# Gates on GpSimd with powers and Newton steps, five y pairs in the key sweep, and w2 steps 0, 6 and 13 as seven products

## The chip, the cores and the metric

The kernel runs on one core of one Trainium2 chip. Its time is device microseconds of that core, and the figure compared is the median of several runs. The profile is one execution taken by the hardware profiler; its span runs from the first instruction to the last.

Names of the engines, as the profile has them: PE is TensorE (matmuls), PEld its weight loads, DVE is VectorE, ACT is ScalarE, POOL is GpSimd, SP is SyncE, which issues most of the DMAs. All matmuls of the large products are float32 split into a high and a low part (fp32r tiles), so that one float32 product costs several matmuls.

## What is computed

```python
x = A_x                                     # 1 x 2048 x 576
g = sigmoid((x * gate_w).sum(-1))           # one gate per token
a = linear_attention(x, wqkv, wo)           # 32 heads of 18
y = layernorm(x)
b = gelu(y @ w1 + b1) @ w2 + b2             # 576 -> 4608 -> 576
out = g * a + (1 - g) * b
```

Here `layernorm` divides by `sqrt(var + 1e-5)`, `gelu` is the tanh form, and the attention uses `phi(t) = where(t > 0, t + 1, exp(t)) + 1e-6` on queries and keys.

## The kernel before

**Stages.** The 2048 tokens are 16 tiles of 128, in two halves of 8 tiles ("sup" 0 and 1). The kernel runs a key sweep over the 16 tiles (projections of keys and queries, `phi`, and the sums of keys by tokens), then a short stage that turns the sums into one weight matrix, then an attention stage over the 16 tiles (`attend`, lines 844 to 861), and then the large part, the two-layer product. Each turn of the key sweep over tile n has three thirds, numbered 3n, 3n+1 and 3n+2; the table `jobs` (line 560) holds closures that are run at the end of a third. So work that is not part of the sweep is put into it by number: the gates of a group of tiles (`gates_in`, `gates_act`, `gates_out`, `share_moments`), and the preparation of normalized inputs, called y, for the first half. In the last three turns of the sweep the queries are left for later, so these turns are shorter.

**The y pairs.** One y pair is two token tiles, one of each 512-token block. `load_pair` (SP) brings the raw rows and their mean and reciprocal deviation; `normal_pair` does four 128x768 DVE operations, `sum_pair` four 128x384 DVE operations; `split_pair` copies high parts on ACT and subtracts them for the low parts on DVE, `split_tails` does the last rows on DVE, and `store_pair` writes the result to HBM. `Y_JOBS` (line 77) gives the thirds. The four pairs of the first half are made in the sweep; the four pairs of the second half are made by `make_y` (line 1287) inside the large part.

**The gates.** `gates_in` (line 362) takes the maximum for the sigmoid and the variance; `gates_act` (line 369) does `Exp` and `Sqrt` on ACT, each with its own table, and an `Exp` on a spare element to bring the first table back; `gates_out` (line 376) does reciprocals and one Newton step for the reciprocal root on DVE. Four groups of two tiles run in the sweep and one group of eight in the attention stage (`MOMENTS`, line 34).

**The large part.** For each half of the tokens, 18 chunks of the 4608 columns are done; a chunk of one half is a step k, 0 to 35. A step has two streams of matmuls. The up stream (`product`) is y times w1, seven products (a Strassen-like scheme of 2x2 blocks) of seven 128x512 matmuls. The down stream is gelu(...) times w2. A step in the set `SEVEN` (line 84) does it as seven products too: 14 units of six 128x288 matmuls (`one_of_seven`). Any other step does it plainly: 8 units of twelve (`plain_unit`). Before the change steps 0, 6, 13 and 35 are plain. The seven products need sums of the blocks of h (`make_sum`) and of w2 (`sum_w2`), and more high and low parts (tiles `h` and `region`). A step in both `SEVEN` and `FIVES` adds some products together in PSUM first, with copies on ACT, and then needs 8 evictions by DVE (`accs<-ps,accs`); a step in `SEVEN` alone needs 12; a plain one 5, and step 0 plain 8.

**The order of the large part** is written by a planner in the kernel (`plan`, line 1420): every operation is an `Op` with an engine, a cost from a table, what it needs and what it gives; a due time is reckoned backward from the matmul streams; the operation to be placed next is chosen by start and due time. `TUNED` (line 89) holds its weights, `ON_DVE` and `DVE_SUMS` say which sums go to DVE and which to POOL (`sum_on`, line 1024). What it gives is a fixed order of instructions for each engine. Two PSUM pairs (banks 6 and 7, banks 4 and 5) take the down units in turn, so a unit waits until the eviction of the unit two before it is done.

Of the kernel before, what the change touches and what calls it, by code (L numbers as in the profile page):

```python
# [17 lines left out]
P = 128  # L18
# [15 lines left out]
MOMENTS = ((0, 2), (2, 4), (4, 6), (6, 8), (8, 16))  # L34
# [1582 lines left out]
```

## Time and profile before

| what | value |
|---|---|
| median of 3 runs | 1095.69 us (1095.6 to 1096.69) |
| span of the profiled execution | 1094.1 us; the page gives no other time for it |
| PE busy | 1087.8 us, 99% of the span, 6694 instructions |
| PEld busy | 996.8 us, 91% |
| DVE busy | 917.2 us, 84% |
| ACT busy | 687.5 us, 63% |
| POOL busy | 235.6 us, 22% |
| mean granted clock of PE | 0.999 of full speed |

A busy time is the union of the instructions' spans. Matmuls are pipelined and each span holds the passage through the array, so that one 128x288 matmul reads 296 ns while the next starts 131 to 132 ns after it; PE at 99% says that matmuls follow each other all the time, not that none of them starts late. The median of the runs lies 1.6 us above the profiled span.

### The profile page before, as it was taken

The numbers are of one execution on the slowest core, as the hardware profiler recorded it, in microseconds if no ns is written. First come the engines' busy times: TensorE is split into PE (matmuls) and PEld (weight loads), VectorE is DVE, ScalarE is ACT, GpSimd is POOL, SyncE is SP. The second block draws the span as 40 slices with busy tenths as digits, with TensorE's granted clock in tenths as the row PEclk, the third lists the DMA queues.
The fourth block names the chain that finished last, engine by engine and source line by source line (L and its number), as shares of the span: only waits on it lengthen the run. The fifth ranks groups of instructions, "written<-read, shape, count | busy, mean of one in ns | idle before, by whom it ended". The sixth has DMA issues, their size and how long they took to land.

```text
span 1094.1 us, 18599 instructions
## 1 busy us (share of the span) xinstructions
PE 1087.8 (99%) x6694; PEld 996.8 (91%) x6694; DVE 917.2 (84%) x1553; ACT 687.5 (63%) x1230; POOL 235.6 (22%) x232
## 2 busy tenths in 40 slices
PE   9999999999999999999999999999999999999998
PEld 9999999999898889988889999989899999999898
DVE  4568784895799999899999997988887888878888
ACT  6677765454667887777877876455545555455552
POOL 2111112531123232332111202121122211221110
PEclk9999999999999999999999999999999999999999
DMA  6466772745745565764556559574444435444432
GB/s 186 128 88 190 171 218 102 286 173 188 252 152 195 184 206 192 235 215 161 199 174 222 195 192 395 174 253 119 138 145 118 130 119 150 132 119 119 135 100 87
DMA packets 109006, 189.72 MB, mean 173 GB/s; under 512 B 8940, under 2 KB 68604, under 8 KB 104818
## 3 DMA queue, kind: packets, MB, share of 16 engines
q1 hardware_dynamic: 108002, 187.78, 53.3%
q8 instruction: 53, 0.87, 0.3%
q10 hardware_dynamic: 720, 0.74, 0.2%
q14 instruction: 39, 0.32, 0.1%
q0 software_dynamic: 192, 0.01, 0.1%
HBM read 121.70 MB, written 66.80 MB: 172 GB/s over the span
## 4 chain that ended last, share of the span: by engine, by line
PE 93%; DVE 3%; DMA 1%; ACT 1%; issue 0%; SPq 0%; ACTq 0%; DVEq 0%
PE ps L120 93%; DVE accs L120 1%; DMA s<-in_wm 0%; DVE h L120 0%; DMA fresh<-in_ue 0%; DMA ystage<-late_acc 0%; ACT u L120 0%; DMA s<-in_we 0%; DVE wp L120 0%; DVE region L120 0%; SPq L120 0%; DVE den L120 0%; DVE fresh L120 0%; DVE ystage L120 0%; DVE u L120 0%
## 5 line engine op out<-in xcount | busy, mean ns | idle before, releaser
L120 PEld LDWEIGHTS ps<-region,h 128*128 128x128 f32 x3072 | 437.8, 188 | 30.1 <-ACT ps L120 4.3
L120 PE MATMUL ps<-region,h 128*128 128x288 f32 x3072 | 457.1, 296 | 1.0 <-DVE region L120 0.4
L120 DVE TENSOR_TENSOR accs<-ps,accs 128x576 f32<-128x576 f32 x330 | 246.1, 753 | 60.9 <-PE ps L120 54.1
L120 PE MATMUL ps<-y,wa 128*128 128x512 f32 x1008 | 257.6, 393 | 0.0
L120 PEld LDWEIGHTS ps<-y,wa 128*128 128x128 f32 x1008 | 180.9, 188 | 30.3 <-ACT ps L120 0.2
L120 POOL TENSOR_TENSOR fresh<-fresh 128x288 f32<-128x288 f32 (+1 forms) x128 | 116.4, 913 | 410.5 <-DMA fresh<-in_w 129.6
L120 PE MATMUL ps<-y,wb 128*128 128x512 f32 x756 | 199.3, 394 | 0.1
L120 DVE TENSOR_TENSOR h<-u,h 128x512 fp32r<-128x512 f32 x240 | 165.9, 704 | 8.7 <-ACT u L120 8.7
L120 PEld LDWEIGHTS ps<-y,wb 128*128 128x128 f32 x756 | 133.9, 188 | 20.9 <-ACT u L120 0.5
L120 ACT ACTIVATE region<-fresh 128x576 fp32r<-128x576 f32 (+1 forms) x132 | 81.3, 625 | 73.5 <-PE ps L120 72.9
L120 PE MATMUL ps<-y 128*128 128x288 f32 (+1 forms) x896 | 125.8, 297 | 0.3 <-DVE y L120 0.2
L120 PEld LDWEIGHTS ps<-y 128*128 128x128 f32 x896 | 122.6, 189 | 1.8 <-DVE y L120 0.4
L120 ACT ACTIVATE ps<-ps 128x576 f32<-128x576 f32 (+1 forms) x127 | 78.7, 621 | 45.0 <-PE ps L120 21.5
L120 POOL TENSOR_TENSOR u<-u 128x512 f32<-128x512 f32 x44 | 57.0, 1296 | 193.5 <-DVE h L120 54.9
L120 DVE TENSOR_TENSOR region<-fresh,region 128x576 fp32r<-128x576 f32 (+1 forms) x132 | 93.8, 723 | 1.1 <-ACT region L120 1.1
L120 ACT ACTIVATE u<-ps 128x512 f32<-128x512 f32 x73 | 43.0, 589 | 68.4 <-PE ps L120 68.2
L120 ACT ACTIVATE h<-u 128x512 fp32r<-128x512 f32 x128 | 73.5, 622 | 10.0 <-DVE u L120 5.5
L120 ACT ACTIVATE h<-u,b1s 128x512 fp32r<-128x512 f32 x73 | 52.6, 722 | 42.6 <-DVE u L120 42.4
L120 PE MATMUL ps<-wp,qt 128*128 128x288 f32 x448 | 63.0, 297 | 0.0
L120 DVE TENSOR_TENSOR u<-ps,u 128x512 f32<-128x512 f32 x74 | 50.4, 683 | 13.5 <-PE ps L120 12.7
L120 PEld LDWEIGHTS ps<-wp,qt 128*128 128x128 f32 x448 | 59.8, 188 | 0.0
L120 DVE TENSOR_TENSOR u<-u 128x512 f32<-128x512 f32 x84 | 58.1, 691 | 1.7 <-POOL u L120 1.1
(137 smaller groups left out, 1052.1 us busy)
## 6 DMA issues: line engine op xcount, KB each, us to landing
w1d<-wa SPq DMA_DIRECT2D x17, 1280.0 KB
wa<-w1d SPq DMA_DIRECT2D x68, 320.0 KB
fresh<-in_w SPq DMA_DIRECT2D x70, 288.0 KB
y<-yd SPq DMA_DIRECT2D x14, 1280.0 KB
w1d<-wb SPq DMA_DIRECT2D x17, 960.0 KB
wb<-w1d SPq DMA_DIRECT2D x51, 320.0 KB
yd<-ystage SPq DMA_DIRECT2D x28, 320.0 KB
fresh<-in_um SPq DMA_DIRECT2D x64, 128.0 KB
```

What stands on the lines that cost most here:

```text
L120: self.last = self.tc.keep_in_program_order(op(*args, **kwargs))
```

## The change

It does these things:

1. The gates move from DVE to POOL: 3 small operations in `gates_in` and 11 in `gates_out`. The reciprocal and the reciprocal root are powers (`OP.pow` with exponents -1 and -0.5 from a small tile), each followed by a Newton step. ACT keeps one `Exp` per group; its `Sqrt` and the spare `Exp` go, and with them 9 of 11 table loads.
2. Gates come in groups of two tiles for ten tiles, and one group of six in the attention stage; before there are four groups of two and one of eight.
3. Five y pairs are made in the key sweep, one every six thirds; the fifth is the first pair of the second half, so `make_y` makes three. The high part of a piece (ACT) is put a third ahead of its low part (DVE).
4. Steps 0, 6 and 13 join `SEVEN`. `FIVES` gains 6, 13 and 17 and loses 16.
5. The planner gets other constants (`HEAR_NS`, a cost for a run of matmuls of one stream, `EACH`), other weights, and a choice of POOL or DVE for every single sum.

```diff
-MOMENTS = ((0, 2), (2, 4), (4, 6), (6, 8), (8, 16))
+MOMENTS = ((0, 2), (2, 4), (4, 6), (6, 8), (8, 10), (10, 16))
-Y_JOBS = ((13, (16, 16, 17, 17), (18, 18, 19, 19), (18, 19, 20, 21)), ...
...
+Y_JOBS = ((9, 14, (16, 16, 17, 17), (18, 18, 19, 19), (18, 19, 19, 20), (19, 20, 20, 21)), ...
...
-SEVEN = set([1, 2, 3, 4, 5, 7, 8, 9, 10, 11, 12, 14, 15, ...
+SEVEN = set([0, 1, 2, 3, 4, 5, 6, 7, 8, 9, 10, 11, 12, 13, 14, 15, ...
...
+HEAR_NS = {"PE": 155, "ACT": 65, "DVE": 65, "POOL": 110, "DMA": 300}
...
-FIVES = set([1, 2, 3, 4, 5, 7, 8, 9, 10, 11, 12, 14, 15, 16])
+FIVES = set([1, 2, 3, 4, 5, 6, 7, 8, 9, 10, 11, 12, 13, 14, 15, 17])
...
     def gates_in(b):
...
-        dve.tensor_scalar(ve, sumsq[:, own], 1 / D, EPS_LN, op0=OP.mult, op1=OP.add)
+        pool.tensor_scalar(ve, sumsq[:, own], 1 / D, EPS_LN, op0=OP.mult, op1=OP.add)
...
     def gates_act(b):
...
         act.activation(g[:, own], g[:, own], AF.Exp, scale=-1.0)
-        act.activation(rstd, ve, AF.Sqrt)
-        if MOMENTS[b][1] < NT:
-            act.activation(tiny, ones[:, 0:1], AF.Exp)
...
     def gates_out(b):
...
+        pool.tensor_scalar(omg[:, own], g[:, own], 1.0, None, op0=OP.add)
+        pool.tensor_tensor(out=g[:, own], in0=omg[:, own], in1=powers[:, 0:1].to_broadcast([P, n]), op=OP.pow)
...
+        pool.tensor_tensor(out=rstd, in0=ve, in1=powers[:, 1:2].to_broadcast([P, n]), op=OP.pow)
+        pool.tensor_tensor(out=vr, in0=rstd, in1=rstd, op=OP.mult)
+        pool.tensor_tensor(out=vr, in0=vr, in1=ve, op=OP.mult)
+        pool.tensor_scalar(vr, vr, -0.5, 1.5, op0=OP.mult, op1=OP.add)
+        pool.tensor_tensor(out=rstd, in0=rstd, in1=vr, op=OP.mult)
...
-    for b, n in enumerate((9, 13, 22, 28)):
-        at(n, gates_in, b)
-        at(n + 1, gates_act, b)
-        at(n + 2, gates_out, b)
-        at(n + 2, share_moments, b)
...
+    for pair, (gated, loaded, normal, added, high, low) in enumerate(Y_JOBS):
+        sup, j = divmod(pair, TPB)
+        at(gated, gates_in, pair)
+        for step in (gates_act, gates_out, share_moments):
+            at(gated + 1, step, pair)
...
-    HEAR = {PE: 155, ACT: 33, DVE: 33, POOL: 78, DMA: 30}
+    HEAR = HEAR_NS
...
-        own = ((what, k, m) in ON_DVE) != ((m, k < NCHUNK) in DVE_SUMS)
+        own = (what, k, m) in ON_DVE
...
-        for j in range(TPB):
+        for j in range(len(Y_JOBS) - TPB, TPB):
             dma(lambda j=j: load_pair(1, j), raw_free["rows"], [("yraw", j)], 5600, 7, each=700)
...
```

How instructions move, at three places.

PE at the start of the large part (`ps<-y,wa` and `ps<-y,wb` are the up stream, `ps<-region,h` the down stream, first of step 0). Before:

```order
L120 MATMUL ps<-y,wa 128x512 x28
L120 MATMUL ps<-y,wb 128x512 x21
L120 MATMUL ps<-y,wa 128x512 x28
L120 MATMUL ps<-region,h 128x288 x12
L120 MATMUL ps<-y,wb 128x512 x7
L120 MATMUL ps<-region,h 128x288 x24
L120 MATMUL ps<-y,wb 128x512 x7
L120 MATMUL ps<-region,h 128x288 x12
```

and with the change:

```order
L120 MATMUL ps<-y,wa 128x512 x28
L120 MATMUL ps<-y,wb 128x512 x21
L120 MATMUL ps<-y,wa 128x512 x25
L120 MATMUL ps<-region,h 128x288 x6
L120 MATMUL ps<-y,wa 128x512 x3
L120 MATMUL ps<-y,wb 128x512 x4
L120 MATMUL ps<-region,h 128x288 x6
L120 MATMUL ps<-y,wb 128x512 x3
```

Units of twelve became units of six, 84 matmuls in the step for 96. In all of the program 3036 of them stand where 3072 stood; no other matmul group changed its count.

POOL in the sweep, from the addition of one tile's keys to the next (`pks<-pks,k`), around the first gates. Before:

```order
L120 MEMSET kvs 126x1152
L120 TENSOR_TENSOR pks<-pks,k 128x576
L120 DMA moments_116<-mr_110 128x4x1
L120 TENSOR_TENSOR pks<-pks,k 128x576 x2
L120 DMA moments_117<-mr_111 128x4x1
```

and with the change:

```order
L120 TENSOR_TENSOR pks<-pks,k 128x576
L120 COPY mr_113<-nmean 128x2
...
L120 TENSOR_SCALAR omg<-g 128x2
L120 TENSOR_TENSOR g<-omg,powers 128x2
L120 TENSOR_TENSOR mt<-omg,g 128x2
L120 TENSOR_SCALAR mt<-mt 128x2
L120 TENSOR_TENSOR g<-g,mt 128x2
L120 TENSOR_SCALAR omg<-g 128x2
L120 TENSOR_TENSOR mr_113<-mt,powers 128x2
...
L120 DMA moments_120<-mr_113 128x4x1
```

Between the addition and the DMA of the moments stand 14 small operations that stood on DVE before.

DVE at the end of the sweep, the last turn but one and the keys of the last (`ys` and `y<-accs` are low parts and tails of a y pair, `xs`, `ks` and `k` belong to the sweep). Before:

```order
L120 SCALAR_TENSOR_TENSOR ks<-k,ks 128x576
L120 TENSOR_TENSOR xs<-xn,xs 128x512
L120 TENSOR_TENSOR xs<-xn,xs 128x64
L120 TENSOR_TENSOR ys_561<-accs,ys_561 128x2x256
L120 SCALAR_TENSOR_TENSOR ys_561<-ys_561,low_rows,accs 128x2x128
L120 TENSOR_TENSOR ys_562<-accs,ys_562 128x2x256
L120 SCALAR_TENSOR_TENSOR ys_562<-ys_562,low_rows,accs 128x2x128
L120 TENSOR_TENSOR y<-accs,y 128x256
L120 SCALAR_TENSOR_TENSOR y<-y,low_rows,accs 128x128
L120 SCALAR_TENSOR_TENSOR k<-ps,e 128x288 x2
```

and with the change:

```order
L120 SCALAR_TENSOR_TENSOR ks<-k,ks 128x576
L120 TENSOR_TENSOR xs<-xn,xs 128x512
L120 TENSOR_TENSOR xs<-xn,xs 128x64
L120 TENSOR_TENSOR accs<-accs 128x384 x4
L120 TENSOR_TENSOR ys_565<-accs,ys_565 128x2x256
L120 SCALAR_TENSOR_TENSOR ys_565<-ys_565,low_rows,accs 128x2x128
L120 TENSOR_TENSOR ys_566<-accs,ys_566 128x2x256
L120 SCALAR_TENSOR_TENSOR ys_566<-ys_566,low_rows,accs 128x2x128
L120 TENSOR_TENSOR ys_567<-accs,ys_567 128x2x256
L120 SCALAR_TENSOR_TENSOR ys_567<-ys_567,low_rows,accs 128x2x128
L120 SCALAR_TENSOR_TENSOR k<-ps,e 128x288 x2
```

The four sums of the pair now stand in this turn, ahead of three low parts with their tails; the four 128x768 operations stand in the turn before.

Counts on DVE, from the order, between the first low part of h and the first operation that finishes an output tile of the first half (`accs<-accs,omg`): evictions `accs<-ps,accs` 133 before and 140 now, low parts of h 121 and 128, of w2 49 and 54 (128x576) and 15 and 18 (128x288), sums of h (`u<-u`) 36 and 40, of w2 (`fresh` 128x288) 32 and 40, of w1 (`fresh` 128x384) 28 and 32; of a y pair `accs<-accs` 128x768 16 and 12, 128x384 16 and 12, `ystage` 128x256 28 and 21, `ystage` 128x128 28 and 21. On POOL, up to its last sum of w1: sums of w1 36 and 32, of w2 20 and 27, of h 20 and 28. In the rest of the program DVE has 0 and 33 sums of w2 and 48 and 34 of h; POOL has 72 and 35 of w2 and 24 and 38 of h.

## Rows read from the trace of the kernel before

**Rows 1.** The page, part 4: shares of the span on the chain that ended last

```profile
PE 93%; DVE 3%; DMA 1%; ACT 1%; issue 0%; SPq 0%; ACTq 0%; DVEq 0%
```

**Rows 2.** Busy time by stretch; in brackets the count of instructions

```profile
core 0: us, PE busy (x) PEld busy (x) DVE busy (x) ACT busy (x) POOL busy (x), PEclk, DMA share, GB/s
25.00:175.00 150.00, 150.00 (x991) 143.45 (x991) 106.41 (x231) 106.42 (x238) 22.82 (x18) 1.00 0.63 164
...
275.00:300.00 25.00, 25.00 (x132) 21.70 (x131) 19.50 (x32) 16.91 (x28) 3.26 (x4) 1.00 0.76 255
300.00:650.00 350.00, 349.21 (x2063) 313.37 (x2062) 336.62 (x564) 268.44 (x444) 86.29 (x80) 1.00 0.56 190
650.00:700.00 50.00, 50.00 (x301) 45.15 (x300) 41.72 (x64) 32.73 (x56) 11.65 (x12) 1.00 0.84 318
...
575.00:600.00 25.00, 25.00 (x157) 23.04 (x156) 25.00 (x43) 19.28 (x31) 3.02 (x3) 1.00 0.60 212
```

**Rows 3.** Timeline of PE, 305 to 312 us: start, length, operation, count

```profile
306.91 1.74 PE L120 MATMUL ps<-region,h 128*128 128x288 f32 x12
308.48 1.76 PE L120 MATMUL ps<-y,wa 128*128 128x512 f32 x7
```

**Rows 4.** Timeline, 540 to 573 us; in square brackets idle time before, and its releaser

```profile
563.55 0.56 DVE L120 TENSOR_TENSOR fresh<-fresh 128x384 f32<-128x384 f32 x1 [1.28 <-DMA fresh<-in_ue]
...
564.05 0.42 PE L120 MATMUL ps<-region,h 128*128 128x288 f32 x2
...
564.83 0.80 PE L120 MATMUL ps<-region,h 128*128 128x288 f32 x4 [0.35 <-DVE region L120]
```

**Rows 5.** Weight loads, 275 to 700 us: busy, mean ns, idle before, what ended it

```profile
L120 PEld LDWEIGHTS ps<-region,h 128*128 128x128 f32 x1553 | 220.5, 188 | 16.3 <-ACT ps L120 4.0 <-DVE region L120 0.6 <-ACT ystage L120 0.4
```

**Rows 6.** Groups of DVE, 300 to 650 us, by form

```profile
L120 DVE TENSOR_TENSOR accs<-ps,accs 128x576 f32<-128x576 f32 x111 | 81.7, 750 | 5.4 <-PE ps L120 5.0
L120 DVE TENSOR_TENSOR h<-u,h 128x512 fp32r<-128x512 f32 x99 | 68.1, 700 | 0.0
L120 DVE TENSOR_TENSOR region<-fresh,region 128x576 fp32r<-128x576 f32 x42 | 34.8, 834 | 0.5 <-ACT region L120 0.5
L120 DVE TENSOR_TENSOR wa<-fresh,wa 128x512 fp32r<-128x512 f32 x30 | 22.2, 740 | 0.9 <-ACT wa L120 0.9
...
L120 DVE TENSOR_TENSOR wb<-fresh,wb 128x768 fp32r<-128x768 f32 x16 | 16.4, 1022 | 2.4 <-ACT wb L120 2.2
...
L120 DVE TENSOR_TENSOR fresh<-fresh 128x288 f32<-128x288 f32 x31 | 14.9, 481 | 0.0
L120 DVE TENSOR_TENSOR accs<-accs 128x768 f32<-128x768 f32 x16 | 14.9, 947 | 0.0
...
L120 DVE TENSOR_TENSOR ystage<-accs,ystage 128x256 fp32r<-128x256 f32 x27 | 11.2, 416 | 0.0
L120 DVE SCALAR_TENSOR_TENSOR ystage<-ystage,low_rows,accs 128x128 fp32r<-128x128 f32 x27 | 10.7, 396 | 2.6 <-ACT ystage L120 2.6
...
L120 DVE TENSOR_TENSOR accs<-accs 128x384 f32<-128x384 f32 x16 | 9.6, 601 | 0.0
```

**Rows 7.** Timeline, 540 to 573 us, a POOL operation and DVE beside it

```profile
546.43 1.03 POOL L120 TENSOR_TENSOR fresh<-fresh 128x384 f32<-128x384 f32 x1 [0.75 <-DVE region L120]
...
546.89 1.12 DVE L120 TENSOR_TENSOR h<-u,h 128x512 fp32r<-128x512 f32 x1
```

**Rows 8.** Timeline of POOL, the key sweep, one tile to the next

```profile
77.91 1.42 POOL L120 TENSOR_TENSOR pks<-pks,k 128x576 f32<-128x576 f32 x1 [5.61 <-DVE k L120]
89.10 1.43 POOL L120 TENSOR_TENSOR pks<-pks,k 128x576 f32<-128x576 f32 x1 [9.77 <-DVE k L120]
```

**Rows 9.** Timeline, 156 to 181 us, the end of the key sweep

```profile
173.22 0.81 DVE L120 TENSOR_TENSOR xs<-xn,xs 128x512 fp32r<-128x512 f32 x2
...
176.88 0.86 PE L120 MATMUL ps<-xs,ks 128*128 128x512 f32 x3
```

**Rows 10.** Tile mr: the matmul that turns the last group's moments

```profile
L120 PE MATMUL ps<-accs,mr x1: 273/273/273, 231.1 to 231.1; 128*16 128x128 f32 x1
```

More of the change, by code (lines that the diff above doesn't have):

```diff
@@ L161, in tile_gated_mix @@
     dve.memset(ones, 1.0)
+    powers = keep.tile([P, 2], F32, name="powers")
+    pool.memset(powers[:, 0:1], -1.0)
+    pool.memset(powers[:, 1:2], -0.5)
     tiny = keep.tile([P, 1], F32, name="tiny")
@@ L428, in tile_gated_mix, with split_pair, high_pair @@
     ys = {}
-    def split_pair(sup, j, part, stage, width=2):
+    def split_pair(*args):
+        high_pair(*args)
+        low_pair(*args[:3])
+    def high_pair(sup, j, part, stage, width=2):
         m0, m1 = width * part, min(width * part + width, 7)
@@ L435, in split_pair, with low_pair @@
         act.activation(to[:, :, 0:3], src, AF.Copy)
+    def low_pair(sup, j, part):
+        _, _, src, to = ys[sup, j, part]
         dve.tensor_sub(to[:, :, 3:5], src[:, :, 0:2], raw(to[:, :, 0:2]))
@@ L557, in tile_gated_mix @@
     y_stages.append(y_place.rearrange("p (m s n) -> p m s n", m=2, s=5))
-    jobs = {n: [] for n in range(3 * NT)}
+    jobs = {n: [] for n in range(3 * NT + 3)}
     def at(n, f, *args):
@@ L1418, in tile_gated_mix, with plan @@
     assert len(in_order) == len(ops)
-    def plan(lag, late, slop, slack, guard, ahead, second=None):
-        second = second or (lag, late, slop, slack, guard, ahead)
+    def plan(lag, late, slop, slack, guard, ahead, second, hold, wait):
         slot, due = {o: n for n, o in enumerate(ups)}, {}
@@ L1444, in plan, with streams @@
         port_at, moved, landed = {e: 0 for e in port_until}, 0.0, []
-        next_up, next_down, shift = 0, 0, 0.0
+        next_up, next_down, shift, run = 0, 0, 0.0, ["", 0]
+        def streams(o):
+            n = round(o.ns / (231.7 if o.by[0] == "up" else 132.3))
+            each, more = EACH[o.by[0]]
+            at_ = run[1] if run[0] == o.by[0] else 0
+            return n, n * each + sum(more[at_:at_ + n])
         def offer(o):
@@ L1493, in choose @@
                     if ta is not None and tb is not None:
-                        if tb <= ta + 100:
+                        if tb <= ta + 100 and not (run[0] == "up" and run[1] < hold and behind < wait and ta <= free[PE]):
                             ta = None
@@ L1523, in plan @@
             s, _, o = min(picks, key=lambda x: x[:2])
-            e, t = o.engine, s + o.tail
+            e, t, ns = o.engine, s + o.tail, o.ns
             if e == PE:
+                n, ns = streams(o)
+                t += ns - o.ns
+                run[:] = o.by[0], n + (run[1] if run[0] == o.by[0] else 0)
                 shift = s - nominal[o]
@@ L1530, in plan @@
                         late, slop, slack, guard = second[1:5]
+                        hold, wait = second[6:8]
                 else:
```

55 lines of the change are left out of this document (28 added, 27 removed).

## The prediction

> **What bounds the kernel now.** I read the chain of waits first: it lies on PE for 93% of the span [rows 1], so time is won by fewer matmuls, by matmuls that start earlier, or not at all. Then the table by stretch [rows 2]: PE is busy without a gap in the key sweep (25 to 175 us) and in the large part, at a granted clock of 1.00. A busy PE hides small delays, since each span holds the passage through the array; so the third view is the timeline of PE, where the spacing is to be read from the starts: twelve 128x288 matmuls take from 306.91 to 308.48, 131 ns each [rows 3].
>
> The fourth view is what makes PE late. At 564.05 two matmuls start, the next ones should come at 564.31 and come at 564.83, 0.52 us late; DVE had waited 1.28 us for a DMA just before [rows 4]. The idle time before the weight loads of the down stream between 275 and 700 us sums what waits cost there: 4.0 for ACT's copies in PSUM, 0.6 for DVE's low parts of w2, 0.4 for others, 5.0 us [rows 5]. That is an upper bound for what PE loses, as loads run ahead of their matmuls. The reader is to see the second resource too: DVE is busy 336.6 of 350 us between 300 and 650 [rows 2]. Of its 13.4 us of idle time there, 5.0 are waits for PE before evictions (DVE is ahead), and the others on the rows are 0.4, 0.5, 0.9, 2.4 and 2.6, with the DMA wait of 1.28 some 8.1 us of waits that it did not choose [rows 4, 6]. In the second half it has room.
>
> A measurement of this kernel can tell about 0.2%, 2.2 us, from no change.
>
> **The change part by part.**
>
> *36 matmuls fewer.* Steps 0, 6 and 13 need 84 down matmuls in place of 96. At 131 ns [rows 3] that is 36 x 0.131 = 4.7 us, and all of it lies on PE, the bound: -4.7. The Trainium skill (TensorE: Matmul & The Clock Gate, section Back-to-back issue gap) gives an isolated gap of N/2.4 + 2.5 ns, 122.5 ns for 288 columns, so an estimate by that page would be 4.4 us for this term; the trace has 131, which I use.
>
> *DVE in the first half of the large part.* The order gives what stands between the first low part of h and the first finished tile. Added: 7 evictions at 0.750, 7 low parts of h at 0.700, 5 of w2 at 0.834 and 3 narrow ones, priced as the sums of the same width at 0.481, 4 sums of h at 0.700 (same columns as the low part), 8 sums of w2 at 0.481, 4 sums of w1 at 0.56 [rows 4, 6]: 5.3 + 4.9 + 4.2 + 1.4 + 2.8 + 3.8 + 2.2 = 24.6 us. Gone with one y pair: 4 x 0.947, 4 x 0.601, 7 x 0.416 and 7 x 0.396 = 3.8 + 2.4 + 2.9 + 2.8 = 11.9 us [rows 6]. Net +12.7 us of DVE, slightly high since operations overlap by a little, while PE's time for the same stretch falls by 4.7.
>
> Does it fit? If everything fell between 300 and 650, DVE would want 336.6 + 12.7 + 8.1 of unchosen waits = 357.4 us where PE wants 350 - 4.7 = 345.3: 12.1 us too much. Against that stand 5.5 us of idle DVE in 275 to 300 and 8.3 in 650 to 700 [rows 2], into which work can move (a good third of the added work belongs to step 0, at the front), and the 8.1 themselves: 21.9 us in all. So the cover is there, but more than half of it is needed. That PE can run beside a full DVE is shown by 575 to 600: DVE 25.00 of 25, PE 25.00 [rows 2]. Bounds of this term beyond the 4.7: all late starts gone, -5.0; nothing moved or saved, 357.4 against the 350 of before, +7.4 and the 4.7 given back, that is +12.1. I take -0.5: the new table reckons a DMA 300 ns later than before instead of 30, which strikes the one 0.52 us late start that a late DMA made [rows 4]; the other late starts I keep, as a fuller DVE makes new ones as readily as it loses old ones.
>
> *The second half of the large part.* DVE gets 33 w2 sums there, and POOL 14 more of h; PE has no late starts of note in it and DVE is not the bound. Cost 0; the room hides it, and with the room gone it would cost what the first half's rows say, 0.481 a sum.
>
> *The fifth y pair in the sweep.* DVE had 106.4 of 150 us there [rows 2]. One pair is 4 x 0.947 + 4 x 0.601 = 6.2, and low parts and tails of about the length of the seven each above, 5.7 at most: +11.9, less the 44 gate operations. In the long turns, 43.6 us of idle DVE hide it. The end is tight: the last three turns have no queries. There DVE gets, in the last turn but one, four sums (2.4) for one tail moved away (0.8), and in the turn before four long operations (3.8) for four sums and about one part (2.4 + 1.2, less one part of the pair now before it): some 2 to 3 us later in all. The last tile's low parts end at 173.22 + 0.81 = 174.03, the matmuls that need them start at 176.88 [rows 9], a cover of 2.85. I take +0.3; bounds 0 and 2.7.
>
> *High part a third ahead of the low.* DVE no longer waits for the ACT copy directly ahead of it; nobody on PE waits for either. Cost 0.
>
> *Gates on POOL.* The trace has no power. A POOL operation takes 1.03 us for 384 columns and 1.42 for 576 [rows 7, 8], 2 ns a column and 0.25 us at no columns. Fourteen operations of two columns: 3.5 us at that price; bound from above, two powers at the cost of a full 576-column operation: 6 us. Behind them wait the next addition of keys, one tile (11.2 us, from 77.91 to 89.10) later [rows 8], and `load_pair` on SP, four thirds of a tile later, 14.9 us. What SP holds behind `load_pair` is input for a tile that is three tiles off. So 0, with 8 us to spare; if a power took over 5 us, SP would be late. In the attention stage the moments' matmul stands at 231.1 [rows 10], two to three tiles behind the gates, and POOL waits there for DVE. Again 0. What ACT gains by fewer table loads is off the chain: 0.
>
> **Sum.** Against the profiled execution, 1094.1: -4.7 - 0.5 + 0.3 = -4.9, so a span of 1089.2. The median of the runs stands 1.6 over that span, so **1090.8 us**.
>
> **The rivals.**
>
> *PE's late starts vanish.* The finer choice of engine for each sum would feed PE in time. For: 5.0 us of waits are few and short [rows 5]. Against: DVE gets fuller. Time: 1095.7 - 4.7 - 5.0 = 1086.0. Chance 0.18.
>
> *DVE takes back the gain.* Part of the 12.1 us finds no place. With 5 to 8 us of it left over, the time is 1090.8 + 0.5 + (2.5 to 6.5): 1093.5 to 1097.8, no difference to be told. For: idle time of DVE at 3.8%, more than half unchosen [rows 2, 6]. Chance 0.15.
>
> *POOL blocks DVE, and DVE becomes the bound.* This one ends on the other side. A subtraction of h that takes 0.700 on average took 1.12 us when it started at 546.89, within a POOL sum that ran from 546.43 to 547.46 [rows 6, 7]: 0.4 lost. POOL's operations in the first half go from 76 to 87 (w1 36 to 32, w2 20 to 27, h 20 to 28), and the h sums are the longest. If each of the 15 added sums blocks DVE by 0.4, that is 6 us, on top of the part of the 12.1 that has no place. It decides from the point where the two together exceed the 4.7 saved plus the 2.2 that can be told: at 8 to 12 us left over the time is 1095.7 - 4.7 + (8 to 12), 1099 to 1103. Against: POOL's operations ran there before, and their cost is inside the means I used. Chance 0.11. The Trainium skill (SBUF — State Buffer, section Who interferes with whom) states this as a rule: a DVE operation with two SBUF inputs and a POOL operation that reads SBUF exclude each other for the whole instruction. By that rule, the trace agrees at 546.89; it would make the added POOL sums a cost in full, not the 0.4 that I read.
>
> *A power is slow.* At over 5 us each, the moments come late, SP stands, and the sweep's inputs with it; each further us costs PE one for every pair, 5 us and more. Nothing in the trace speaks for it. Chance 0.02, slower.
>
> **How the numbers follow.** The forecast keeps 0.54, from about 1088 to 1093.4. The first rival lies at 1086.0, the second up to 1097.8, the last two beyond. The range takes in the first rival and the lower half of the second: 1086.0 to 1096.0; outside stay the upper part of the second (0.06), what lies below 1086.0 (0.02) and the slower ones (0.13). Faster by over 0.2% (under 1093.5): 0.54 + 0.18 and a little of the second, 0.74. Same: 0.14. Slower: 0.12.
>
> **What would show it.** Right: 3036 down matmuls at 131 to 132 ns; idle before weight loads from 275 to 700 us between 4 and 5 us; DVE at 98% or more from 300 to 650; idle of DVE in 650 to 700 smaller than 8.3; POOL's gates under 6 us a group; no wait of SP for moments. Wrong: PE's matmuls spaced apart in the first half with DVE at 25.00 of 25 in every stretch (DVE is the bound); the h subtractions well over 0.700 on average (POOL blocks it); a gap on PE at the end of the sweep of over 1 us.

## The result, and the profile after

The change made the kernel slower, by 0.3%: a median of 1099.84 us (1095.4 to 1101.45, 13 runs) against 1096.25 us before (1095.28 to 1097.31, 13 runs on the same chip), ratio 1.003 [1.0021, 1.0039]. The profiled execution of the changed kernel took 1098.14 us, with a span of 1096.4 us. Its page, part 1, and from part 4 the shares of the chain [rows 1]:

```profile
PE 1085.2 (99%) x6658; PEld 992.1 (90%) x6658; DVE 940.7 (86%) x1553; ACT 690.2 (63%) x1231; POOL 273.6 (25%) x307
...
PE 88%; DVE 5%; DMA 3%; ACT 1%; SPq 1%; issue 1%; POOL 1%; ACTq 0%; DVEq 0%
```

The chain leaves PE for DVE, DMA, SP and POOL, 12% of the span in place of 7%. Where, the starts of PE's first matmuls of each stage tell. Three of them from the timeline of PE, changed kernel: the first sum of keys, the first product of ones that ends the sweep, and the first of the large part.

```profile
27.22 3.02 PE L120 MATMUL ps<-ks,xs 128*128 128x512 f32 x15
...
188.75 1.13 PE L120 MATMUL ps<-pks,ones 128*128 128x288 f32 x4
...
280.87 6.54 PE L120 MATMUL ps<-y,wa 128*128 128x512 f32 x28
```

Before the change the same three stand at 26.32, 180.61 and 272.65. Read in this way, in us:

| kernel | to the first sum | key sweep | to the large part | large part | its first half | after the last matmul's start |
|---|---|---|---|---|---|---|
| before | 26.3 | 154.3 | 92.0 | 817.5 | 394.6 | 4.0 |
| changed | 27.2 | 161.5 | 92.1 | 811.9 | 390.0 | 3.7 |

So in these two executions the large part gained 5.6 us, where the prediction had 5.2 (4.7 + 0.5), and the key sweep lost 7.2, where it had 0.3. The 5.6 is at the upper end. Ten of the runs below (all but 4, 6, 7 and 10) have the changed kernel's order of instructions in the large part; in these eleven profiles it takes 811.9 to 814.5 us, 3.0 to 5.6 less than before. The first half, in which steps 0, 6 and 13 lie, varies little: 389.9 to 390.4 us, 4.2 to 4.6 less than the 394.6 before. The 0.9 ahead of the sweep belongs to the execution: in the profiles of all runs that part takes 26.1 to 27.4 us.

**The large part.** The busy times by stretch that answer to [rows 2]:

```profile
core 0: us, PE busy (x) PEld busy (x) DVE busy (x) ACT busy (x) POOL busy (x), PEclk, DMA share, GB/s
25.00:175.00 150.00, 147.22 (x961) 139.64 (x960) 105.95 (x190) 93.84 (x214) 55.67 (x88) 0.99 0.66 166
...
300.00:650.00 350.00, 349.78 (x2064) 314.59 (x2063) 347.64 (x587) 279.78 (x461) 91.95 (x87) 1.00 0.55 187
```

The weight loads of the down stream from 275 to 700 us, as in [rows 5]:

```profile
L120 PEld LDWEIGHTS ps<-region,h 128*128 128x128 f32 x1500 | 214.3, 188 | 14.6 <-ACT ps L120 1.5 <-ACT pks L120 0.5 <-ACT u L120 0.3
```

Three groups of DVE from 300 to 650 us, as in [rows 6]:

```profile
L120 DVE TENSOR_TENSOR accs<-ps,accs 128x576 f32<-128x576 f32 x120 | 87.7, 748 | 1.7 <-PE ps L120 1.2
L120 DVE TENSOR_TENSOR h<-u,h 128x512 fp32r<-128x512 f32 x109 | 75.4, 708 | 0.0
...
L120 DVE TENSOR_TENSOR fresh<-fresh 128x288 f32<-128x288 f32 x36 | 16.3, 452 | 0.3 <-POOL fresh L120 0.3
```

And PE's timeline for the spacing of the down matmuls, as in [rows 3]:

```profile
313.10 1.75 PE L120 MATMUL ps<-region,h 128*128 128x288 f32 x12
314.69 1.09 PE L120 MATMUL ps<-y,wa 128*128 128x512 f32 x4
```

Twelve down matmuls take 1.59 us, 132 ns each. DVE is busy for 347.64 of 350 us, and yet the idle time before weight loads that waits ended fell from 5.0 to 2.3 us (1.5 + 0.5 + 0.3). DVE's own idle time is nearly gone with it. How little of that reached PE, the first half above tells: it gained what 36 matmuls cost.

**The key sweep.** In 25 to 175 us PE is idle for 2.78 us and its clock is 0.99. The timeline of PE at the end of the sweep, changed kernel (in square brackets the idle time before, and its releaser):

```profile
164.59 3.22 PE L120 MATMUL ps<-ks,xs 128*128 128x512 f32 x16
170.30 5.49 PE L120 MATMUL ps<-y 128*128 128x288 f32 x28 [2.50 <-DVE k L120]
175.63 0.84 PE L120 MATMUL ps<-xs,ks 128*128 128x512 f32 x3
176.31 3.22 PE L120 MATMUL ps<-ks,xs 128*128 128x512 f32 x16
181.14 2.12 PE L120 MATMUL ps<-y 128*128 128x288 f32 x14 [1.61 <-DVE k L120]
```

In the kernel before, the same sixteen matmuls are followed by the next group after 3.06 us (170.10 to 173.16), and 28 of that group take 3.72 us (173.16 to 176.88). Here the next group comes 5.71 and 4.83 us after the sixteen: two gaps of 2.65 and 1.77 us. And the 28 after the first gap take 5.33 us: 1.6 us more. That is the clock, as the busy times by stretch show:

```profile
170.00:171.00 1.00, 0.70 (x5) 0.73 (x6) 1.00 (x4) 0.00 (x0) 0.00 (x0) 1.00 0.96 368
171.00:172.00 1.00, 1.00 (x9) 1.00 (x8) 0.39 (x2) 0.58 (x1) 0.47 (x1) 0.88 1.00 344
172.00:173.00 1.00, 1.00 (x6) 1.00 (x5) 0.77 (x1) 1.00 (x3) 0.95 (x1) 0.50 1.00 249
```

2.65 + 1.6 + 1.77 are 6.0 of the 7.2 us; the rest are three gaps of 0.2 to 0.3 us one, two and three pairs earlier, and smaller ones. What DVE did ahead of the first gap (timeline of DVE, changed kernel):

```profile
165.65 1.95 DVE L120 TENSOR_TENSOR accs<-accs 128x768 f32<-128x768 f32 x2 [3.75 <-DMA accs<-in_xe]
167.84 1.95 DVE L120 TENSOR_TENSOR accs<-accs 128x768 f32<-128x768 f32 x2 [0.23 <-DMA accs<-in_xe]
169.71 0.45 DVE L120 SCALAR_TENSOR_TENSOR k<-ps,e 128x288 f32<-128x288 f32 x1
```

What SP issued ahead of that (its own timeline):

```profile
148.40 0.54 SPq L120 DMA_DIRECT2D xn<-in_x  x1
154.85 0.38 SPq L120 DMA_DIRECT2D yd<-ys  x1
157.31 0.33 SPq L120 DMA_DIRECT2D accs<-moments  x1
```

And POOL ahead of SP (timeline of POOL):

```profile
137.28 0.72 POOL L120 COPY mr<-nmean 128x2 f32<-128x2 f32 x1
...
140.36 0.23 POOL L120 TENSOR_SCALAR omg<-g 128x2 f32<-128x2 f32 x1 [1.55 <-ACT g L120]
140.66 0.72 POOL L120 TENSOR_TENSOR g<-omg,powers 128x2 f32<-128x2 f32 x1
...
142.31 0.95 POOL L120 TENSOR_SCALAR omg<-g 128x2 f32<-128x2 f32 x1
...
145.60 0.91 POOL L120 TENSOR_TENSOR mr<-mr,mt 128x2 f32<-128x2 f32 x1
146.81 0.87 POOL L120 DMA_DIRECT2D moments<-mr  x1 [0.30 <-POOL mr L120]
```

Read from below: the fifth pair's gates take POOL from 137.28 to 146.51, 9.2 us. The store of the moments is issued at 146.81 and lands at 157.3, 10.5 us later. SP, free since 155.2, reads them at 157.31 and then issues the raw rows; DVE gets them at 165.65. DVE has stood 3.75 us by then, and behind its four long operations, in order, stands `k`, for which PE waits. (SP's standing makes up 2.1 of these 3.75 us; the rest is left by the landing of the rows themselves.) At the second gap DVE comes from two turns of full work; and ACT (the next fence) waits 2.24 us for a store of y before a copy, behind which stands the exponent that `k` needs:

```profile
179.22 0.52 ACT L120 ACTIVATE y<-accs 128x384 fp32r<-128x384 f32 x1 [2.24 <-DMA yd<-y]
```

### The profile page after: what moved, and what is told of

The parts are those of the page before. It is cut to its first block, busy times and chain, and to the rows that moved or that the text cites. A ratio compares the mean times of both kernels' runs of the same rounds, so it can differ in the third digit from the quotient of the medians.

```text
span 1096.4 us, 18608 instructions
## 1 busy us (share of the span) xinstructions
PE 1085.2 (99%) x6658; PEld 992.1 (90%) x6658; DVE 940.7 (86%) x1553; ACT 690.2 (63%) x1231; POOL 273.6 (25%) x307
## 4 chain that ended last, share of the span: by engine, by line
PE 88%; DVE 5%; DMA 3%; ACT 1%; SPq 1%; issue 1%; POOL 1%; ACTq 0%; DVEq 0%
PE ps L120 88%; DVE accs L120 2%; SPq L120 1%; DMA yd<-y 1%; DMA moments<-mr 1%; DMA accs<-in_xe 1%; DVE h L120 1%; DMA s<-in_we 0%; DVE region L120 0%; DMA s<-in_wm 0%; DVE y L120 0%; DVE u L120 0%; DVE wa L120 0%; DVE fresh L120 0%; DVE wp L120 0%
## 5 line engine op out<-in xcount | busy, mean ns | idle before, releaser
L120 PEld LDWEIGHTS ps<-region,h 128*128 128x128 f32 x3036 | 431.9, 188 | 27.8 <-ACT ps L120 1.5
L120 PE MATMUL ps<-region,h 128*128 128x288 f32 x3036 | 449.8, 295 | 0.3
L120 DVE TENSOR_TENSOR accs<-ps,accs 128x576 f32<-128x576 f32 x340 | 251.3, 752 | 32.1 <-PE ps L120 26.9
L120 DVE TENSOR_TENSOR h<-u,h 128x512 fp32r<-128x512 f32 x249 | 174.1, 724 | 8.6 <-ACT u L120 7.3
L120 POOL TENSOR_TENSOR fresh<-fresh 128x288 f32<-128x288 f32 (+1 forms) x94 | 83.8, 894 | 316.8 <-DVE wa L120 51.7
L120 POOL TENSOR_TENSOR u<-u 128x512 f32<-128x512 f32 x66 | 87.4, 1324 | 285.1 <-DVE h L120 83.7
L120 ACT ACTIVATE region<-fresh 128x576 fp32r<-128x576 f32 (+1 forms) x138 | 84.8, 624 | 86.4 <-PE ps L120 85.1
L120 ACT ACTIVATE ps<-ps 128x576 f32<-128x576 f32 (+1 forms) x137 | 85.1, 622 | 50.8 <-PE ps L120 34.7
L120 ACT ACTIVATE h<-u 128x512 fp32r<-128x512 f32 x140 | 81.7, 621 | 4.9 <-DVE u L120 4.3
L120 ACT ACTIVATE h<-u,b1s 128x512 fp32r<-128x512 f32 x73 | 52.7, 722 | 11.1 <-DVE u L120 11.0
L120 DVE TENSOR_TENSOR accs<-accs 128x768 f32<-128x768 f32 (+1 forms) x64 | 49.6, 779 | 9.1 <-DMA accs<-in_xe 8.3
```

The lines of the kernel that those rows point to most:

```text
L120: self.last = self.tc.keep_in_program_order(op(*args, **kwargs))
```

## The experiments

Theory 1 was, from this: the loss is the lateness of the fifth pair's moments (first gap, with the clock) and its work in turns that are too short (second gap); the gates on POOL, the landing of two transfers and the table's places act together. Rivals are named with each run. The kernel before was run beside each group: 1095.97 us (17 runs) for the first four, 1095.5 (15, of which one took 1520.54), 1095.84 (23), 1095.57 and 1096.02 (13 each) for the later ones; the changed kernel was not run again beside them.

**1. The seventh piece in the half of the stage buffer that the pair before did not use** (ACT need not wait for the store).

```
-            at(when, high_pair, sup, j, part, lambda part=part: y_stages[part])
+            at(when, high_pair, sup, j, part, lambda part=part, pair=pair: y_stages[part][:, pair % 2:] if part == 3 else y_stages[part])
```

> The changed kernel, with the seventh piece of each y pair in the half of its stage that the pair before did not use, so that ACT's last high part no longer waits for the store of the pair before. Theory 1 (DVE and ACT, both in order, stand at the fifth pair's data at the end of the sweep, and PE waits for the keys queued behind): the second gap on PE (1.8 us near 179) goes, the first (2.7 us near 167) stays; 1.5 to 3 us faster than the changed kernel, about 1097.5. Rival 2 (the short last turns have too much DVE work whatever waits there are): the gap stays, since DVE itself is late; within 1 us of the changed kernel. Rival 3 (GpSimd's gates are the cause): within 1 us.

Measured: 1094.79 us (1092.62 to 1097.81, 10 runs), ratio 0.9989 [0.998, 0.9999]. The median fell by 5 us, where 1.5 to 3 were expected, and of the gaps the reverse came. ACT's wait is gone, but the second gap stays (timeline of PE):

```profile
172.16 3.23 PE L120 MATMUL ps<-ks,xs 128*128 128x512 f32 x16
177.33 2.91 PE L120 MATMUL ps<-y 128*128 128x288 f32 x20 [1.94 <-DVE k L120]
```

DVE from the fifth pair's rows on:

```profile
163.12 4.02 DVE L120 TENSOR_TENSOR accs<-accs 128x768 f32<-128x768 f32 x4 [1.53 <-DMA accs<-in_xe]
```

From 163.12 to the `k` at 176.82 DVE has no wait for data but one of 0.85 us for ACT's `ks`: the second gap is DVE's amount of work in two short turns, not the store. The first gap fell to 0.5 us, since the store of the moments, issued at 146.89, had landed by 155.52; and without the long gap the clock stayed at 1.00. So the first gap hangs on how long that store takes, 8.6 us here and 10.5 above. Why it took less is not shown: the edit holds for the seventh piece of every pair, so ACT's waits and the stores of y ahead of it move too. The mean granted clock of the other executions shows that this is more than one lucky store: it is 0.998, as in the profile with the slow stretch, in 10 of the changed kernel's 13 executions and in 2 of the 10 of run 1, and 1.000 in the others.

**2. The fifth pair's work one to two places later; 3. the same with edit 1; 9. two of its copies later still.**

```
-(33, 38, (40, 40, 41, 41), (42, 42, 43, 43), (42, 43, 43, 44), (43, 44, 44, 45))
+(33, 38, (42, 42, 42, 42), (43, 43, 43, 44), (44, 44, 45, 45), (45, 45, 46, 46))
...
+(33, 38, (42, 42, 42, 42), (43, 43, 43, 44), (44, 45, 45, 45), (45, 45, 46, 46))
```

> The changed kernel, with the fifth pair's four long DVE operations moved from thirds 40 and 41 to 42, behind the next tile's keys, and its sums and parts one to two thirds later. Theory 1: DVE no longer stands at rows that have not landed with keys queued behind it; the gap near 167 and the halved clock after it go (2.7 us and about 1.5 us), the second gap may stay; 3 to 4.5 us faster than the changed kernel, about 1096. Rival 2: the same work in fewer turns makes the last tile's keys later: no gain or slower, 1099 to 1102. Rival 3: within 1 us of the changed kernel.

> Both edits together. Theory 1: both gaps and the slow clock go, 5 to 7 us faster than the changed kernel, 1093 to 1095, and faster than the kernel before by 1.5 to 3.5 us, as the large part is 5.6 us shorter in the trace. Rival 2: 2 us faster than the changed kernel at most. Rival 3: within 1 us of the changed kernel.

> The version with the fifth pair's work later (1092.25), with the second and third of its copies on ACT (high parts) one place later as well. There the last gap on PE before the end of the sweep is 0.59 us at 172.9: DVE's keys wait for ACT, which had taken the second copy (171.45, 0.85 us) ahead of the keys' exponent. Theory 1: that gap goes, 0.4 to 0.6 us, and 1091.7 comes out, not to be told from 1092.25. Rival (DVE's eight long operations from 166.42 to 172.60 are themselves the bound there): no change at all in that gap.

Measured: 1092.25 us (1091.6 to 1094.62, 7 runs), ratio 0.9971 [0.996, 0.9982]; with edit 1 1092.1, ratio 0.9966 [0.9952, 0.998]; with the copies later still 1091.82 (1090.84 to 1093.42, 5 runs), ratio 0.9965 [0.9952, 0.9977]. The three can't be told apart; all beat both kernels, the kernel before by 0.3%. One edit of places took both gaps but for 0.6 and 0.25 us, the timeline of PE in run 2:

```profile
170.04 3.22 PE L120 MATMUL ps<-ks,xs 128*128 128x512 f32 x16
173.68 3.98 PE L120 MATMUL ps<-y 128*128 128x288 f32 x28 [0.42 <-DVE k L120]
177.50 0.85 PE L120 MATMUL ps<-xs,ks 128*128 128x512 f32 x3
178.19 3.26 PE L120 MATMUL ps<-ks,xs 128*128 128x512 f32 x16
181.50 1.21 PE L120 MATMUL ps<-pks,ones 128*128 128x288 f32 x4
```

The sweep takes 155.2 us (155.1 in run 9), the large part 812.9. The gain over the changed kernel, 7.6 us, was twice what I had expected of run 2: the second gap, of which I had said that it may stay, went too, and the changed kernel's median lies 1.7 us above the profiled execution from which I had worked. In run 9 the 0.6 us are gone as expected, but PE starts late by about as much in the groups behind, and the sweep is shorter by 0.1 us only.

**5. The gates back on DVE and ACT, at the changed kernel's places; 11. the same on top of run 2; 6. the gates on POOL alone, in the kernel before.**

```
-        pool.tensor_tensor(out=rstd, in0=ve, in1=powers[:, 1:2].to_broadcast([P, n]), op=OP.pow)
+        act.activation(rstd, ve, AF.Sqrt)
...
+        dve.reciprocal(rstd, rstd)
```

> The changed kernel with the gates' operations back on DVE and ACT as before the change, at the changed kernel's places in the sweep. Theory 1: the moments are issued 4 to 5 us sooner than at 146.8, since DVE's operations of two columns are short, so the rows are no longer late; first gap 0.5 us at most, no slow clock: about 1096. Rival (POOL has no part in it, the pair is gated and loaded at the wrong place): no change, 1099.8. Rival 3 (the operations that come back to DVE and ACT, 44 and the table loads, are themselves too much for the sweep): over 1100.

> The version with the fifth pair's work later (1092.25), with the gates back on DVE and ACT. With the changed kernel's places the gates on DVE gave 1095.13 against 1099.84. Theory 1 (gates on POOL cost only through the moments' lateness, which the later places cover): within 1 us of 1092.25. Rival (gates on POOL cost by themselves, by holding up DVE): 1091 or less. Rival (the operations on DVE and the table loads on ACT cost something in the sweep): over 1094.

> The kernel before with the gates on POOL and nothing else. The prediction costed that edit at 0: 1096 within 1 us. Theory 1: the kernel before loads its pairs three to seven places after the gates, and the first and third pair have the least; their moments come 5 us later than now (9.5 us of POOL in place of DVE's short operations), so the first pair's rows can be late by up to 2 us: 1096 to 1098. Rival (gates on POOL cost by themselves in each of five groups): over 1099.

Measured: 1095.13 us (1091.92 to 1096.6, 10 runs), ratio 0.9994 [0.9984, 1.0004]; on run 2 1092.46, ratio 0.9969 [0.9959, 0.998]; alone 1096.3 (1095.11 to 1096.72, 10 runs), ratio 1.0002 [0.9993, 1.0011]. Timelines of POOL, SP, DVE and PE in run 5:

```profile
142.50 0.77 POOL L120 DMA_DIRECT2D moments<-mr  x1 [7.23 <-DVE mr L120]
...
153.03 0.42 SPq L120 DMA_DIRECT2D accs<-moments  x1
...
160.54 1.95 DVE L120 TENSOR_TENSOR accs<-accs 128x768 f32<-128x768 f32 x2 [0.91 <-DMA accs<-in_xe]
...
175.42 3.98 PE L120 MATMUL ps<-y 128*128 128x288 f32 x28 [2.19 <-DVE k L120]
```

The store leaves at 142.50, 4.3 us earlier, SP is not held, DVE waits 0.91 in place of 3.75 us, and the first gap is gone; the second (2.19 us of idle PE) stays. The median is 4.7 us below the changed kernel's. So at these places the gates on POOL cost most of the loss, through the moments that come late; but 4 of the 10 executions of run 5 have a mean granted clock of 0.998, so in these a long gap may be left, and no profile of them shows where. Where the places leave them room, POOL's gates cost nothing: run 11 is not to be told from run 2, and run 6 not from the kernel before. Nor do they gain anything there.

**8. The fifth pair's gates one tile earlier; 12. the same on top of run 2; 13 and 14. as 12, with the store alone later.**

```
-(33, 38,
+(30, 38,
```

```
-        for step in (gates_act, gates_out, share_moments):
+        for step in (gates_act, gates_out):
             at(gated + 1, step, pair)
+        at(34 if pair == 4 else gated + 1, share_moments, pair)
...
+        at(36 if pair == 4 else gated + 1, share_moments, pair)
```

> The changed kernel with the fifth pair's gates and its store of the moments one tile earlier (place 30 of the sweep in place of 33); nothing else moves. Theory 1 (the moments come late: gates on POOL 9.5 us, landing 10.5 us, only then SP can issue the rows): SP is then held by the store ahead of it alone, which it issued at 154.85, so the rows are issued at 155.2 in place of 157.3; the first gap on PE shrinks from 2.66 us to about 0.5 and the granted clock does not fall to 0.50 behind it (1.5 us); the second gap (1.8) stays. Time about 1096.2, and the runs lie within 3 us of each other in place of 6. Rival 2 (the last short turns hold too much work for DVE whenever the rows come): no change, 1099.8.

> The version with the fifth pair's work later (1092.25), with the fifth pair's gates one tile earlier. In the changed kernel that edit gave 1100.91: the fifth pair's rows were in time, but 3.13 us of idle PE opened at the fourth pair, whose first operation on DVE stood 4.35 us without a releaser in the profile. If that comes from the fifth pair's gates and their store beside the fourth pair's loads: it comes here too, 3 to 5 us, 1095 to 1097. If it came from a single late transfer: 1092.3.

> The version with later work and the fifth pair's gates one tile earlier (1099.98), but with the store of the fifth pair's moments back at its place of the changed kernel (34); the gates' operations stay early. In the run without that, DVE stood 5.87 us (140.3 to 146.15) before the fourth pair's rows, while the store, issued at 135.91, was in flight for 10.7 us and the DMA engines, busy at 59 to 85%, moved 21 to 56 GB/s. Theory 4 (the store of the moments, 2 KB in pieces of 4 bytes, slows the loads that fall beside it): the stall is gone, 1092.3 within 1. Rival (the gates' operations on POOL at that place are what holds DVE up): the stall stays, 1097 to 1100.

> As e13, which did not do what it was for: POOL had nothing to wait for between the gates and place 34, so it issued the store at 137.89, 2 us later than e12, and the wait at the fourth pair grew to 8.84 us. Here the store stands behind POOL's next addition of keys, which waits for DVE until about 147, after the fourth pair's rows have landed; the gates' operations stay one tile early. Theory 4 (the small store slows the loads that are in flight with it): the wait at the fourth pair is gone, 1092.3 within 1.2, with runs within 3 us of each other. Rival (the gates' operations on POOL at that place hold DVE up): the wait stays, 1096 to 1100.

Measured: 8 gave 1100.91 us (1099.25 to 1102.06, 4 runs), ratio 1.0049 [1.0033, 1.0065]; 12 gave 1099.98 (1094.36 to 1101.16, 10 runs), ratio 1.0031 [1.0019, 1.0042]; 13 gave 1096.32 (1093.01 to 1102.88, 10 runs), ratio 1.001 [0.9991, 1.0029]; 14 gave 1094.02 (1092.13 to 1095.37, 10 runs), ratio 0.9981 [0.9972, 0.9991]. A miss for theory 1 in run 8: the fifth pair's rows were in time, DVE waited 0.29 us for them, but now DVE stood ahead of the fourth pair's. The timeline of DVE in run 12:

```profile
146.15 3.81 DVE L120 TENSOR_TENSOR accs<-accs 128x768 f32<-128x768 f32 x4 [5.87 <-issue]
```

The busy times by stretch of run 12, of DVE alone:

```profile
core 0: us, DVE busy (x), PEclk, DMA share, GB/s
...
140.00:142.00 2.00, 0.28 (x1) 1.00 0.59 21
142.00:144.00 2.00, 0.00 (x0) 1.00 0.85 42
144.00:146.00 2.00, 0.00 (x0) 1.00 0.76 56
```

The fourth pair's rows were issued from 131.53 on; the fifth pair's moments, 2 KB, at 135.91, and that store took 10.7 us to land. While it was in flight the DMA engines were busy and moved little, and DVE waited 5.87 us for the pair's rows. Run 14 leaves POOL's gates early and puts only the store behind POOL's next addition of keys, at 147.68. The timeline of DVE in run 14:

```profile
140.34 1.95 DVE L120 TENSOR_TENSOR accs<-accs 128x768 f32<-128x768 f32 x2 [0.47 <-DMA accs<-in_xe]
```

The same stretches in run 14:

```profile
140.00:142.00 2.00, 1.63 (x2) 1.00 0.72 224
142.00:144.00 2.00, 1.65 (x3) 1.00 0.98 344
144.00:146.00 2.00, 2.00 (x5) 1.00 1.04 415
```

The wait at the fourth pair is 0.47 us. (The 224 to 415 GB/s are not of the same transfers as in run 12: here SP issued two stores of y from 140.92 on, there they left at 146.08. The wait of DVE is what compares.) Run 13 missed and did not separate the two: POOL had nothing to wait for, so the store left at 137.89, with a wait of 8.84 us behind it in the profiled execution, the slowest of the ten; five executions lie at 1093.0 to 1095.4 us and five at 1097.3 to 1102.9. Runs 12 and 14 differ in the place of the store alone. So it is the store, not the gates' operations, that must not fall beside a pair's loads; how it slows them, the profile does not show. Run 14 stays 1.8 us behind run 2, more than was expected, with a gap of 1.56 us left at 175.65. That is the moments once more (timelines of SP and DVE, run 14):

```profile
156.60 0.33 SPq L120 DMA_DIRECT2D accs<-moments  x1
...
167.64 0.83 DVE L120 TENSOR_TENSOR xs<-xn,xs 128x512 fp32r<-128x512 f32 x2 [1.05 <-ACT xs L120]
```

The store, issued at 147.68, landed 8.9 us later, and SP, free since 153.57, stood until then. Behind the pair it held a tile's input `xn`, issued at 162.24 (159.45 in run 2), for which ACT waited 1.59 us and DVE behind it 1.05.

**4. Steps 0, 6 and 13 as seven products in the kernel before; 10. the three steps undone in run 2; 7. four pairs in the sweep, four in the large part.**

```
-SEVEN = set([1, 2, 3, 4, 5, 7, 8, 9, 10, 11, 12, 14, 15,
+SEVEN = set([0, 1, 2, 3, 4, 5, 6, 7, 8, 9, 10, 11, 12, 13, 14, 15,
```

Run 4 also has 6 and 13 in `FIVES`; run 10 is the reverse of the two lines; run 7 drops the last entry of `Y_JOBS` and has `MOMENTS` as before.

> The kernel before, with steps 0, 6 and 13 as seven products (6 and 13 in the group with shared products) and nothing else: 36 matmuls fewer, four y pairs in the sweep, the old planner. If DVE's room is what decides in the first half: 24.6 us more DVE work against 27 us of idle time of which 8 cannot be used and 4.7 us less time, so 5 to 10 us too much, 1097 to 1102, with PE waiting for evictions and low parts. If only the count of matmuls decides: 4.7 us faster than before, about 1091.5.

> The version with the fifth pair's work later (1092.25), with w2 steps 0, 6 and 13 back to eight products: 36 matmuls more, and less work for DVE; the rest of the new table of the order stays. Theory 1 (the large part gained by fewer matmuls alone): large part 812.9 + 4.7 = 817.6, time 1097.0. Rival (the new table gains by itself): large part below 816, time below 1095.5. Rival (the table fits only the steps for which it was made, as the steps did not fit the old table): PE waits through the order, time over 1100.

> The changed kernel without the fifth pair in the sweep; the fifth is made in the large part, with three others, as before the change. Theory 1: the sweep's two gaps are gone, 161.5 us back to 154 to 155; but DVE gets 11.9 us in the first half of the large part, where it is busy for 347.6 of 350 us. If the room at both ends holds it, 1093; if it finds no place, up to 1100 with the first half longer than 390.0 by the difference. Rival (the sweep is longer because of the new places of the parts and of the gates, not because of the fifth pair): the sweep stays above 158, time 1097 or more.

Measured: 4 gave 1134.19 us (1131.85 to 1135.65, 4 runs), ratio 1.035 [1.0334, 1.0365]; 10 gave 1098.93 (1097.28 to 1100.03, 6 runs), ratio 1.0029 [1.0017, 1.0042]; 7 gave 1110.09 (1109.93 to 1113.1, 4 runs), ratio 1.014 [1.0124, 1.0157]. Run 4 (up to 1102 expected) and run 7 (up to 1100 by theory 1) missed by far; run 10 met theory 1 in the large part and lies 1.9 us above it in time. Busy times from 300 to 650 us in run 4:

```profile
300.00:650.00 350.00, 327.71 (x1846) 286.85 (x1845) 328.86 (x533) 252.32 (x420) 95.41 (x90) 0.97 0.52 178
```

The same stretch in run 7:

```profile
300.00:650.00 350.00, 338.61 (x1952) 299.54 (x1952) 343.64 (x577) 266.49 (x441) 84.92 (x81) 0.99 0.55 189
```

Run 10's large part takes 817.2 us, 4.3 more than run 2's 812.9, and its first half 395.1, 4.7 more than run 2's 390.4: the 36 matmuls, as the prediction had them, and nothing besides that the new table would have won. Between the profiled spans lie 5.3 us, the 4.3, 0.8 ahead of the sweep and 0.3 in it. Between the medians lie 6.7: four of run 10's six executions took 2.4 to 2.9 us more than their span, against 1.7 or 1.8 in the other runs; why is not explained. Run 4's first half takes 434.6 us, 40 more than before, with PE and DVE both idle: the steps can't be had with the old order as it stands. Run 7's sweep is back at 154.8, so the fifth pair is what lengthens it; but its first half takes 409.3, 19.3 more than the changed kernel's. With this order, the three steps fit only once the fifth pair's 11.9 us of DVE had left that half; whether another order would have had room for both was not tried, nor why 11.9 us of DVE cost 19.3.

## Why the prediction was wrong

The forecast was 1090.8 us, with a range from 1086.0 to 1096.0; the median is 1099.84, 9.0 above. Of these, 6.9 lie in the key sweep (7.2 for 0.3), 1.7 in that the changed kernel's median lies that far above its profiled execution, and 0.4 in all else. The step that failed is the cover behind the gates on POOL, with the fifth pair's end of the sweep beside it.

- **36 matmuls fewer: right.** -4.7 forecast; run 10's first half takes 4.7 more than run 2's, with 132 ns a matmul.
- **DVE in the first half: right that the work fits, 0.5 too hopeful.** The work found its place: DVE 347.64 of 350 us, above the 98% named, and the h subtractions at 0.708 us against 0.700. The waits before weight loads fell to 2.3 us, not 4 to 5. But the first half gained 4.2 to 4.6 us, no more than the matmuls: the -0.5 for late starts does not show, and 2.7 us less of waits before loads won PE nothing that can be told. That the whole large part came out at -5.6 against -5.2 is luck: the 1.0 above the first half's 4.6 lies in the second half, which varies by 2.5 us between executions of the same order. Nothing of the rival "PE's late starts vanish" came but its waits. The rivals "DVE takes back the gain" and "POOL blocks DVE, and DVE becomes the bound" did not come. (The price of the former does not follow: 5 to 8 us left over, added as the latter adds them, give 1096 to 1099, and 1090.8 + 0.5 + 2.5 is 1093.8.) Blocking is there where the operations are short: most of POOL's gate operations of two columns take 0.19 to 0.23 us, but 0.95 and 0.91 when they start within DVE's long operations (142.31 and 145.60 above). The Trainium skill (SBUF — State Buffer, section Who interferes with whom) has a DVE instruction with two SBUF inputs contend with a POOL instruction that reads SBUF, by an exclusive lock; the trace agrees with that here, and the price is paid by POOL.
- **Gates on POOL, "So 0, with 8 us to spare": this is the step that failed.** It cost the first gap and the slow clock behind it, 2.65 + 1.6 = 4.3 us, and run 5, without it, is 4.7 faster. Three lengths were wrong or missing. The group took 9.2 us, not 3.5 to 6: the powers were cheap (0.72), but the fourteen operations start one after the other, wait 1.55 for ACT, and three short ones take 0.87 to 0.95 beside DVE. The landing of the store, 10.5 us, was not counted at all, although the tile of the store had shown 9.9 to 11.1 us in the kernel before. And the rows need 8.3 us more from SP's issue to DVE. The way from the gates to DVE is 9.2 + 0.3 + 10.5 + 8.3, some 28 us; the cover counted ended at SP. Two signs named for a right forecast, gates under 6 us a group and no wait of SP for moments, failed with it. Nor was what SP holds behind `load_pair` safe: in run 14 it was a tile's input for which ACT waited. The Trainium skill (DMA: Bandwidth & Descriptors, section Anatomy of one DMA — SWDGE (gpsimd) path) gives 2.0 us plus bytes over 436 GB/s for a DMA that POOL issues; an estimate by that page would be 2.0 us for these 2 KB. The traces have 7.5 to 12.6, and the measurement decides.
- **The end of the sweep, "+0.3; bounds 0 and 2.7": wrong in what was looked at.** I compared DVE's end with the last tile's need and found a cover of 2.85 us. What came late was the tile before, since DVE works in order and stood at a transfer ahead of `k` (the first gap), and then the next tile's `k`, behind too much work of DVE (the second gap, 1.77 us). The wrong sign named in the text, a gap on PE of over 1 us at the end of the sweep, came twice.
- **"High part a third ahead": 0, right for the cost, not for "nobody on PE waits".** ACT's copy did stand 2.24 us ahead of an exponent that PE needed, but run 1 shows that the gap is there without it.
- **"A power is slow"** (0.02) had the right chain (moments late, SP stands, PE waits) and the wrong cause; a power takes 0.7 to 1.5 us with two columns. The chain needed no slow power, only the landing that I had left out, and deserved far more.

With the fifth pair's work at later places (runs 2, 3 and 9) the change gives what was forecast, to 1.0 to 1.5 us: 1091.82 to 1092.25 against 1090.8.

## What to carry to other kernels

When work moves to another engine or to an earlier place, follow its result to the reader on the bound engine's path, with every transfer's landing in the sum, and not to the next instruction that names it; the cover is what is left at the end of that whole way. On an engine that works in order, a wait for data costs whoever stands behind it, so put an operation that reads a transfer behind the work that PE needs next. A small store can delay large loads beside it: move it on its own before you move what it belongs to. And hold a stage's gain against a forecast only over several executions: the same order of the large part took 811.9 to 814.5 us here, a spread of 2.6 us around a term of 0.5 that it seemed to confirm.

## What the runs showed of the hardware

- The store of the moments, 2 KB from 128 partitions, took 7.5 to 12.6 us to land. While it was in flight beside a pair's loads in run 12, the DMA engines were 59 to 85% busy and moved 21 to 56 GB/s, and DVE waited 5.87 us for the loads; with the store behind them in run 14 it waited 0.47.
- After PE's idle time of 2.50 us before 170.30 the granted clock was 0.50 (1.2 GHz) in 172 to 175 us. After the second gap of the changed kernel (1.61 us of idle PE), of run 1 (1.94) and of run 5 (2.19) the profiles show 1.00 throughout.
- A POOL power of two columns took 0.69 to 1.52 us in the changed kernel, one of six columns 1.36 and 1.86.
- Three of POOL's operations of two columns that started within a DVE operation of 128x768 (142.31, 144.65 and 145.60) ended 0.05 us after it and took 0.87 to 0.95 us; others of the group, with no such DVE operation beside them, took 0.19 to 0.23.
